# Attention with a low-rank mixer and an MLP on one core: diagonal score blocks first, early key copies, column groups, and transposes of q, k and u by DMA

## Chip, cores, metric

One core of one Trainium2 chip. The metric is the device time of one execution in microseconds (us). Each version was run several times, beside runs of the kernel before on the same chip. A run over 1.5% above the fastest of its kernel counts as slow.

Names: PE is TensorE, the matrix engine; DVE, ACT and POOL are VectorE, ScalarE and GpSimd; SP (SyncE) here only issues DMAs, as POOL does for the loads. SBUF is the on-chip memory for tiles, PSUM the one that PE writes its results to, from where ACT or DVE copy them out.

## The reference, cut to what matters

```python
# q, k, v: (4 batches, 8 heads, 768, 64), float32
scores = q @ k^T / 8 + bias            # keep: key in the first 8, or 0 <= row - column < 96
a      = softmax(scores)               # bias = -slope[head] * distance
x      = (a @ v), heads side by side   # (4, 768, 512)
h      = (x^T @ U @ V)^T               # mixes rows; rank 32
u      = x + h
out    = u + relu(u @ w_ch1) @ w_ch2   # 512 -> 2048 -> 512
```

Because of the band, a query block of 128 rows needs only two key blocks: its own (the "diagonal" block) and the one before, into whose first 32 rows the global keys are copied.

## The kernel before

Heads are worked in pairs: 4 pairs a batch, 16 in all. `kT` and `qT` hold keys and queries transposed, `kP` is the key copy for the previous blocks with the global keys put in, `vp` the same for v. Matrix products take fp16. After pair 3, MLP "units" (four matmuls of 512 columns) of the finished batch are put between the steps of the next pairs: `fill(f)` issues `f` of them, and a pair has eight such slots. What matters below is that DMAs put on one queue are issued in the order of the program: in the timeline after, the transposes of pair 8 come out behind its vp copies (from 84.89 us to 88.96 us).

```python
ORDER = [(1, t) for t in range(1, NSB)] + [(0, t) for t in range(1, NSB)] + [(0, 0)]   # 1: needs kP
CH = [list(range(0, 4)), list(range(4, 8)), list(range(8, 11))]      # three groups of score blocks

def transposes(i, which):               # q or k of pair i: 12 PE transposes of 128 x 64
    ...
        nc.tensor.matmul(tp[64*hi:64*hi+64, sb*P:(sb+1)*P], stg[:, hi, sb], ident16, is_transpose=True, ...)
    ...                                 # qT copied out of PSUM by ACT, kT by DVE

def v_prev(i):                          # vp of pair i, on the SP queue; waits for v
    nc.sync.dma_start(vp[G:P], vh[G:P, :, 0:NPB]); ...   # 3 DMAs

def mix_tmp(i):                         # U-product: accumulates into 32 partitions
    for c in range(NSB):
        nc.tensor.matmul(tmp_ps[0:R], u16[:, c], x16[:, c], start=(c == 0), stop=(c == NSB - 1))
    nc.vector.tensor_copy(tmp16, tmp_ps[0:R])

def mix_t(i):                           # u transposed: 6 PE transposes, copied to uT by DVE
    ...

for i in range(NPAIR, NP):              # pairs 4 to 15
    v_prev(i + 2)
    scores(i + 1, 0)
    fill(f)
    av(i)
    norm(i)
    fill(f)
    scores(i + 1, 1)
    cast_x(i)                           # ACT: x to fp16
    fill(f)
    mask(i + 1, 0)
    transposes(i + 2, 0)
    fill(f)
    mix_tmp(i)
    scores(i + 1, 2)
    fill(f)
    mix_h(i, nc.gpsimd)                 # V-product, u = x + h, cast to fp16
    fill(f)
    transposes(i + 2, 1)
    mask(i + 1, 1)
    k_prev(i + 2, nc.gpsimd)            # kP of pair i + 2
    fill(f)
    if i % 2 == 0 and i + 4 < NP:
        load(i + 4, 2)                  # q, k, v of two pairs, on the POOL queue, cast to fp16
    mix_t(i)
    ...
    fill(f)
```

The softmax here doesn't subtract the row's maximum and nothing guards it: scores larger than these inputs give would overflow.

Of the kernel before, what the change touches and what calls it, by code (L numbers as in the profile page):

```python
# [10 lines left out]
FP16 = mybir.dt.float16  # L11
I32 = mybir.dt.int32
AF = mybir.ActivationFunctionType
ALU = mybir.AluOpType
# [3 lines left out]
def kernel(  # L18
# [13 lines left out]
    nc = tc.nc  # L32
# [14 lines left out]
    TT = 512  # L47
    D1 = D + 1
    KEEP = False
    assert NG <= G and NL <= P - G + 1 and NPAIR == NDC  # L50
    qk_scale = 1.0 / math.sqrt(D)
    BIG = -30000.0
# [1 line left out]

    cst = ctx.enter_context(tc.tile_pool(name="cst", bufs=1))
    big = ctx.enter_context(tc.tile_pool(name="big", bufs=1))
    stp = ctx.enter_context(tc.tile_pool(name="stp", bufs=6))
    qkp = ctx.enter_context(tc.tile_pool(name="qkp", bufs=3))
    epp = ctx.enter_context(tc.tile_pool(name="epp", bufs=2))
    smp = ctx.enter_context(tc.tile_pool(name="smp", bufs=2))  # L60
# [14 lines left out]
    def ps_tp(name, dtype, cols):  # L75
        return psum.tile([P, cols], dtype, name=name, tag="tp", bufs=1)
# [10 lines left out]
    vp16 = big.tile([P, VPR, 2, NPB, D1], FP16, name="vp16")  # L87

    NP = B * NPAIR
    stage = {}  # L90
    xs = {}

# [12 lines left out]
    def load_v(i0, n):  # L105
# [5 lines left out]
            .rearrange("(m p) d -> p m d", p=P),  # L111
        )

    def load(i0, n):
        load_qk(i0, n)
        load_v(i0, n)

    w1v = moe_w_ch1.rearrange("(c p) n -> p c n", p=P)
# [24 lines left out]
    nc.gpsimd.iota(reli, pattern=[[-1, 2 * P]], base=0, channel_multiplier=1)  # L143
    load_v(0, 1)
    load(1, 1)
    load(2, 2)
    u16 = cst.tile([P, NSB, R], FP16, name="u16")
    nc.gpsimd.dma_start(u16, moe_U.rearrange("(c p) r -> p c r", p=P))
    v16w = cst.tile([R, S], FP16, name="v16w")
    nc.gpsimd.dma_start(v16w, moe_V)  # L150
    load_w1()


# [32 lines left out]
    u16s = {}  # L186
    obs = {}
    tmps = {}
    NSTART = NPAIR + 2

    def transposes(i, which):
        if i >= NP:
            return
        stg = stage.pop((i, which))
        if i < NSTART:
            bank = ps_mm("tpb")
            keep_busy(bank, 8 if i == 0 and which == 0 else 1)
            tp = bank.bitcast(FP16)[:, 0:NSB * P]
        else:
            tp = ps_tp("tp", FP16, NSB * P)  # L200
        for sb in range(NSB):
            for hi in range(2):
                nc.tensor.matmul(  # L203
                    tp[64 * hi:64 * hi + 64, sb * P:(sb + 1) * P], stg[:, hi, sb],
                    ident16, is_transpose=True,
                    start=(sb == 0), stop=(sb == NSB - 1),
                )
        tv = tp.rearrange("p (n c) -> p c n", n=NSB)
        if which == 0:
            qT = qkp.tile([P, S], FP16, name="qT", tag="qT")  # L210
            nc.scalar.activation(qT.rearrange("p (c n) -> p c n", n=NSB), tv, AF.Copy)  # L211
            qTs[i] = qT
        else:
            kT = qkp.tile([P, NSB, P], FP16, name="kT", tag="kT")
            nc.vector.tensor_copy(  # L215
                kT.rearrange("p n c -> p (n c)").rearrange("p (c n) -> p c n", n=NSB), tv,
            )
            kTs[i] = kT

    def k_prev(i, eng):  # L220
# [21 lines left out]
                )  # L242


    ORDER = [(1, t) for t in range(1, NSB)] + [(0, t) for t in range(1, NSB)] + [(0, 0)]
    CH = [list(range(0, 4)), list(range(4, 8)), list(range(8, 11))]

    def scores(i, ci):
        if i >= NP:
            return  # L250
        qT, kT, kP = qTs[i], kTs[i], kPs[i]
        if ci == 0:
            probs[i] = epp.tile([P, 2, NBK, P], FP16, name="ep", tag="ep")
        ep = probs[i]
        idx = CH[ci]
        n = len(idx)
        scs = [ps_sc("sc") for _ in range(2)]
        if i < NPAIR:
            keep_busy(scs[0], 1)
        for j, bi in enumerate(idx):  # L260
            prev, t = ORDER[bi]
            for hi in range(2):
                r = slice(64 * hi, 64 * hi + 64)
                lhsT = kP[r, t - 1] if prev else kT[r, t]
                nc.tensor.matmul(  # L265
                    scs[hi][:, j * P:(j + 1) * P], lhsT, qT[r, t * P:(t + 1) * P],
                    start=(j == 0), stop=(j == n - 1),
                )
        for hi in range(2):
            nc.scalar.activation(  # L270
                ep[:, hi, idx[0]:idx[0] + n].rearrange("p n c -> p (n c)"),
                scs[hi][:, 0:n * P], AF.Exp, scale=qk_scale,
            )

    def mask(i, part):
        if i >= NP:
            return
        hp = i % NPAIR
        ep = probs[i]
        eb = expb[:, 2 * hp:2 * hp + 2]  # L280
        j0, m = ((0, 2), (NPB, 1))[part]
        blk = ep[:, :, j0:j0 + NPB]
        nc.vector.tensor_tensor(  # L283
            blk, blk, eb[:, :, m:m + 1].broadcast_to((P, 2, NPB, P)), ALU.mult,
        )
        if part == 1:
            nc.vector.tensor_tensor(
                ep[:, :, NBK - 1], ep[:, :, NBK - 1], eb[:, :, 0], ALU.mult
            )

    def av(i):
        obs[i] = ps_ob("ob")
        ep = probs.pop(i)
        for hi in range(2):
            ob = obs[i][:, 512 * hi:512 * hi + NSB * D1].rearrange("p (n d) -> p n d", n=NSB)
            for t in range(NSB):
                if t == 0:
                    nc.tensor.matmul(
                        ob[:, 0], ep[:, hi, NBK - 1], v16[:, i % VR, hi, 0],
                        start=True, stop=True,  # L300
                    )
                    continue
                nc.tensor.matmul(  # L303
                    ob[:, t], ep[:, hi, t - 1], vp16[:, i % VPR, hi, t - 1],
                    start=True, stop=False,
                )
                nc.tensor.matmul(  # L307
                    ob[:, t], ep[:, hi, NPB + t - 1], v16[:, i % VR, hi, t],
                    start=False, stop=True,
                )  # L310

# [20 lines left out]
    def mix_tmp(i):  # L332
        x16 = x16s.pop(i)
        tmp_ps = ps_tp("tmp_ps", FP32, P)
        for c in range(NSB):
            nc.tensor.matmul(  # L336
                tmp_ps[0:R], u16[:, c], x16[:, c], start=(c == 0), stop=(c == NSB - 1),
            )
        tmp16 = smp.tile([R, P], FP16, name="tmp16", tag="tmp16")
        nc.vector.tensor_copy(tmp16, tmp_ps[0:R])  # L340
        tmps[i] = tmp16

    def mix_h(i, eng):
# [16 lines left out]
    def mix_t(i):  # L360
        b, hp = divmod(i, NPAIR)
        uu = u16s.pop(i)
        tpu = ps_tp("tpu", FP16, S)
        for st in range(NSB):
            nc.tensor.matmul(
                tpu[:, st * P:(st + 1) * P], uu[:, st], ident16, is_transpose=True,
                start=(st == 0), stop=(st == NSB - 1),
            )
        nc.vector.tensor_copy(uT[:, hp, b * S:(b + 1) * S], tpu)
# [66 lines left out]
    for i in range(NPAIR):  # L436
        last = i == NPAIR - 1
        v_prev(i + 2)
        scores(i + 1, 0)
        av(i)  # L440
        norm(i)
        scores(i + 1, 1)
        if i > 0:
            mix_t(i - 1)
        cast_x(i)
        mask(i + 1, 0)
        if not last:
            transposes(i + 2, 0)
            mix_tmp(i)
            scores(i + 1, 2)  # L450
            transposes(i + 2, 1)
            mix_h(i, nc.vector if i == 0 else nc.gpsimd)
            if i + 2 < NPAIR:
                masks_of(i + 2)
            if i == 0:
                v_prev(1)
            mask(i + 1, 1)
            k_prev(i + 2, nc.vector if i == 0 else nc.gpsimd)
        else:
            mix_tmp(i)  # L460
            scores(i + 1, 2)
            mix_h(i, nc.vector)
            transposes(i + 2, 0)
            transposes(i + 2, 1)
            mix_t(i)
            mask(i + 1, 1)
            k_prev(i + 2, nc.gpsimd)
        if i == 0:
            load(4, 2)
        if i == 1:  # L470
            load_w2()
        if i == 2:
            load(6, 2)
# [7 lines left out]

    for i in range(NPAIR, NP):
        if i % NPAIR == 0:
            f = max(1, len(mlp_q) // (8 * NPAIR))
        v_prev(i + 2)
        scores(i + 1, 0)
        fill(f)
        av(i)
        norm(i)
        fill(f)  # L490
        scores(i + 1, 1)
        cast_x(i)
        fill(f)
        mask(i + 1, 0)
        transposes(i + 2, 0)
        fill(f)
        mix_tmp(i)
        scores(i + 1, 2)
        fill(f)
        mix_h(i, nc.gpsimd)  # L500
        fill(f)
        transposes(i + 2, 1)
        mask(i + 1, 1)
        k_prev(i + 2, nc.gpsimd)
        fill(f)
        if i % 2 == 0 and i + 4 < NP:
            load(i + 4, 2)
        mix_t(i)
        if i % NPAIR == NPAIR - 1:
            queue_batch(i // NPAIR)  # L510
        fill(f)
# [37 lines left out]
```

## Time and profile before

| | before |
|---|---|
| median | 291.84 us (3 runs, 290.54 to 291.88) |
| span of the profiled run | 289.3 us |

From the profile page of the kernel before, the busy times and two rows of the span in 40 slices (each digit the busy share of one slice in tenths; PEclk the granted TensorE clock):

```profile
PE 252.7 (87%) x2144; PEld 129.0 (45%) x2144; DVE 149.3 (52%) x239; ACT 104.4 (36%) x185; POOL 61.2 (21%) x80
...
PE   2564585698899999999999999988999999999994
...
PEclk9999999999999999999999999999999999999998
```

PE is the busiest engine, but not evenly. The windows view of the same kernel cuts the span into five stages: the start (pairs 0 to 3 without MLP), pairs 4 to 7, 8 to 11, 12 to 15, and the tail of MLP alone. Columns: window, its length, busy us (and instructions) of PE, PEld (weight loads), DVE, ACT, POOL, then granted clock, DMA share, GB/s.

```profile
0.00:58.70 58.70, 32.76 (x423) 24.23 (x424) 34.43 (x64) 27.12 (x49) 25.02 (x36) 1.00 1.28 165
58.70:111.40 52.70, 49.58 (x482) 24.52 (x481) 31.41 (x48) 23.90 (x43) 14.79 (x18) 1.00 0.59 78
111.40:184.00 72.60, 72.25 (x597) 34.88 (x596) 39.21 (x60) 26.55 (x48) 14.80 (x18) 1.00 0.45 70
184.00:228.50 44.50, 41.37 (x391) 20.57 (x390) 26.99 (x42) 17.23 (x31) 6.64 (x8) 1.00 0.10 33
228.50:289.30 60.80, 56.70 (x257) 24.81 (x255) 17.28 (x25) 9.55 (x16) 0.00 (x0) 0.98 0.11 39
```

In the start PE is busy 32.8 of 58.7 us: it waits. In the three stages of pairs 4 to 15 it is busy 93 to over 99% of the time. Pairs 4 to 7 and 12 to 15 have one unit per slot, pairs 8 to 11 two.

The waits of PE in the start, before (engine, line, who was waited for: us in sum, times, longest):

```profile
PE sc L265 <- POOL kP L226: 8.4, 3, 3.4
PE sc L265 <- DVE kP L226: 6.8, 3, 3.6
```

The first score group needs kP, which is made last. The waits of the SP queue, before: SP stands still for v, at the vp copies, for a quarter of the span.

```profile
SPq L238 <- DMA v_84<-in_v_dram: 69.3, 4, 19.1
```

Last, PE's timeline in one pair of 4 to 7, before (start, duration, line, operation; in brackets the idle time before it and who ended it):

```profile
78.94 0.49 PE L336 MATMUL tmp_ps<-x_1024,u_111 128*32 128x128 f16 x6 [0.69 <-ACT qT L211]
79.37 0.34 PE L265 MATMUL sc<-qT,kT 64*128 64x128 f16 x6
79.64 1.04 PE L381 MATMUL hps<-uT,w_16_81 128*128 128x512 f16 x4
80.61 0.50 PE L348 MATMUL h_ps<-tmp_1061,v16w 32*128 32x128 f16 x6
81.05 1.04 PE L381 MATMUL hps<-uT,w_16_81 128*128 128x512 f16 x4
82.01 0.53 PE L203 MATMUL tp<-ident_93,qkst 128*64 128x128 f16 x12
82.47 1.04 PE L381 MATMUL hps<-uT,w_16_81 128*128 128x512 f16 x4
```

The modelled durations overlap, so the cost of a group is read from start to start: the U-product took 0.43 us (79.37 - 78.94), the V-product 0.44, twelve k transposes 0.46. PE waited 0.69 us ahead of the U-product here.

### The profile page before, as it was taken

The numbers are of one execution on the slowest core, as the hardware profiler recorded it, in microseconds if no ns is written. First come the engines' busy times: TensorE is split into PE (matmuls) and PEld (weight loads), VectorE is DVE, ScalarE is ACT, GpSimd is POOL, SyncE is SP. The second block draws the span as 40 slices with busy tenths as digits, with TensorE's granted clock in tenths as the row PEclk, the third lists the DMA queues.
The fourth block names the chain that finished last, engine by engine and source line by source line (L and its number), as shares of the span: only waits on it lengthen the run. The fifth ranks groups of instructions, "written<-read, shape, count | busy, mean of one in ns | idle before, by whom it ended". The sixth has DMA issues, their size and how long they took to land.

```text
span 289.3 us, 5035 instructions
## 1 busy us (share of the span) xinstructions
PE 252.7 (87%) x2144; PEld 129.0 (45%) x2144; DVE 149.3 (52%) x239; ACT 104.4 (36%) x185; POOL 61.2 (21%) x80
## 2 busy tenths in 40 slices
PE   2564585698899999999999999988999999999994
PEld 1343464454444444444444444544444444444441
DVE  5646736736665665564554635666655432123221
ACT  2753552444644234533146331446431032013100
POOL 8820137102430721060200701120301100000000
PEclk9999999999999999999999999999999999999998
DMA  8999979960971294039120291200011200210021
GB/s 86 176 191 211 175 98 192 191 71 6 125 64 39 30 207 107 2 39 162 73 81 4 21 180 73 69 18 2 0 39 37 75 0 0 75 73 0 0 73 74
DMA packets 47975, 22.68 MB, mean 78 GB/s; under 512 B 31408, under 2 KB 44368, under 8 KB 47952
## 3 DMA queue, kind: packets, MB, share of 16 engines
q0 software_dynamic: 36656, 13.73, 41.1%
q1 hardware_dynamic: 11296, 8.63, 10.2%
q8 instruction: 17, 0.28, 0.4%
q14 instruction: 6, 0.05, 0.1%
HBM read 27.46 MB, written 6.29 MB: 117 GB/s over the span
## 4 chain that ended last, share of the span: by engine, by line
PE 64%; DVE 11%; ACT 10%; POOL 8%; DMA 3%; issue 2%; POOLq 0%; DVEq 0%
PE cps L399 25%; PE hps L381 21%; PE sc L265 6%; ACT ep L270 4%; DVE kT L215 4%; DMA u_111<-in_moe_U_dram 3%; DVE x_sb L353 3%; PE tmp_ps L336 3%; POOL kP L225 3%; PE h_ps L348 2%; PE ob L303 2%; PE ob L307 2%; ACT qT L211 1%; POOL qkst L98 1%; POOL uu L357 1%
## 5 line engine op out<-in xcount | busy, mean ns | idle before, releaser
L381 PE MATMUL hps<-uT,w_16_81 128*128 128x512 f16 x384 | 94.1, 383 | 0.4
L399 PE MATMUL cps<-w_16_82,htr 128*128 128x512 f16 x384 | 90.4, 380 | 0.0
L270 ACT ACTIVATE ep<-sc 128x512 f16<-128x512 f32 (+1 forms) x96 | 48.7, 560 | 90.0 <-PE sc L265 90.0
L381 PEld LDWEIGHTS <-w_16_81 128*128 128x128 f16 x384 | 34.2, 98 | 40.2 <-issue 5.1
L399 PEld LDWEIGHTS <-htr 128*128 128x128 f16 x384 | 34.4, 98 | 38.5
L386 ACT ACTIVATE htr<-hps 128x512 f16<-128x512 f32 x48 | 28.7, 598 | 62.5 <-PE hps L381 61.9
L388 DVE TENSOR_SCALAR htr<-hps 128x512 f16<-128x512 f32 x48 | 33.0, 688 | 34.6 <-PE hps L381 34.6
L357 POOL CAST uu<-x_sb 128x768 f16<-128x768 f32 x14 | 13.1, 935 | 146.9 <-DVE x_sb L353 146.9
L406 DVE TENSOR_TENSOR osb<-cps,x_sb 128x512 f32<-128x512 f32 x24 | 16.6, 690 | 34.0 <-PE cps L399 34.0
L283 DVE TENSOR_TENSOR ep<-ep,expb 128x1280 f16<-128x1280 f16 x32 | 26.2, 818 | 7.4 <-ACT ep L270 7.4
L265 PE MATMUL sc<-qT,kP 64*128 64x128 f16 x160 | 11.6, 249 | 16.2 <-POOL kP L226 8.4
L353 DVE TENSOR_TENSOR x_sb<-x_sb,h_ps 128x768 f32<-128x768 f32 x16 | 15.2, 951 | 16.6 <-PE h_ps L348 16.6
L203 PEld LDWEIGHTS <-qkst 128*64 128x64 f16 x384 | 14.6, 130 | 15.8 <-issue 10.2
L265 PEld LDWEIGHTS <-kP 64*128 64x128 f16 x160 | 5.9, 104 | 27.6 <-POOL kP L226 13.0
L319 DVE RECIPROCAL rcp<-ob 128x12 f32<-128x12 f32 x16 | 3.7, 232 | 25.2 <-PE ob L307 25.2
L225 POOL COPY kP<-kT 128x480 f16<-128x480 f16 x13 | 13.0, 1000 | 15.4 <-DVE kT L215 15.4
L320 DVE TENSOR_TENSOR x_sb<-ob,rcp 128x768 f32<-128x768 f32 x16 | 15.3, 957 | 0.6
L303 PE MATMUL ob<-vp_85,ep 128*128 128x65 f16 x160 | 15.0, 209 | 0.0
L307 PE MATMUL ob<-v_84,ep 128*128 128x65 f16 x160 | 14.9, 209 | 0.0
L203 PE MATMUL tpb<-ident_93,qkst 128*64 128x128 f16 x144 | 10.0, 314 | 5.3 <-DMA qkst<-in_q_dram 4.8
L303 PEld LDWEIGHTS <-ep 128*128 128x128 f16 x160 | 13.1, 108 | 1.6 <-issue 0.3
L307 PEld LDWEIGHTS <-ep 128*128 128x128 f16 x160 | 13.2, 109 | 0.0
(112 smaller groups left out, 204.1 us busy)
## 6 DMA issues: line engine op xcount, KB each, us to landing
out_dram<-osb SPq DMA_DIRECT2D x24, 256.0 KB, 2.0
qkst<-in_q_dram POOLq DMA_DIRECT2D x7, 384.0 KB, 5.6
qkst<-in_k_dram POOLq DMA_DIRECT2D x7, 384.0 KB, 8.3
v_84<-in_v_dram POOLq DMA_DIRECT2D x7, 384.0 KB, 11.3
w_16_81<-in_moe_w_ch_dram POOLq DMA_DIRECT2D x2, 1024.0 KB, 15.8
w_16_82<-in_moe_w_ch_dram POOLq DMA_DIRECT2D x2, 1024.0 KB, 13.4
vp_85<-v_84 SPq DMA_DIRECT2D x14, 121.9 KB, 3.0
vp_85<-v_84 SPq DMA_DIRECT2D x28, 20.3 KB, 2.5
```

What stands on the lines that cost most here:

```text
L203: nc.tensor.matmul(tp[64 * hi:64 * hi + 64, sb * P:(sb + 1) * P], stg[:, hi, sb], ident16, is_transpose=True, start=(sb == 0), stop=(sb == ...
L225: eng.tensor_copy(kP[:, :, G:P], kT[:, 0:NPB, G:P])
L265: nc.tensor.matmul(scs[hi][:, j * P:(j + 1) * P], lhsT, qT[r, t * P:(t + 1) * P], start=(j == 0), stop=(j == n - 1),)
L270: nc.scalar.activation(ep[:, hi, idx[0]:idx[0] + n].rearrange("p n c -> p (n c)"), scs[hi][:, 0:n * P], AF.Exp, scale=qk_scale,)
L283: nc.vector.tensor_tensor(blk, blk, eb[:, :, m:m + 1].broadcast_to((P, 2, NPB, P)), ALU.mult,)
L303: nc.tensor.matmul(ob[:, t], ep[:, hi, t - 1], vp16[:, i % VPR, hi, t - 1], start=True, stop=False,)
L307: nc.tensor.matmul(ob[:, t], ep[:, hi, NPB + t - 1], v16[:, i % VR, hi, t], start=False, stop=True,)
L353: nc.vector.tensor_tensor(xp, xp, hps[:, 0:S].rearrange("p (n c) -> p n c", n=NSB), ALU.add)
L381: nc.tensor.matmul(hh, w1_16[:, dc, jt * P:(jt + 1) * P], uT[:, dc, t0:t0 + TT], start=(dc == 0), stop=(dc == NDC - 1),)
L386: nc.scalar.activation(htr[:, jt], hh, AF.Relu)
L388: nc.vector.tensor_scalar_max(htr[:, jt], hh, 0.0)
L399: nc.tensor.matmul(cps, htr[:, jc, tt * P:(tt + 1) * P], w2_16[:, jc], start=(jc == 0), stop=(jc == NJC - 1),)
```

## The change

The intent: take work off PE, which bounds pairs 4 to 15, and shorten the chain that bounds the start. Diagonal blocks need only kT, so they go first and kP may come later. kT is copied by ACT. The U-product goes to four column groups of the array, and the V-product then sums over 128 instead of 32 partitions. q and k from pair 6 on, and u from batch 1 on, are transposed by DMA from one SBUF tile to another; for that q and k are loaded row by row, into four buffers.

```diff
+    NSTART = NPAIR + 2
+    def load_qk_natural(i):
+        for which, src in enumerate((q, k)):
+            stg = stp.tile([P, NSB, 2, D], FP16, name="qkn", tag="qkn", bufs=4)
+            for hi in range(2):
+                nc.gpsimd.dma_start(stg[:, :, hi], src[b, 2*hp + hi].rearrange("(n p) d -> p n d", p=P))
...
     def transposes(i, which):
+        if DT and i >= NSTART:
+            dst = qkp.tile([P, NSB, P], FP16, name="qkT", tag="qT" if which == 0 else "kT")
+            nc.sync.dma_start_transpose(dst, stg.rearrange("p n h d -> p (n h d)"))
+            ...
+            return
...
-            nc.vector.tensor_copy(kT..., tv)
+            nc.scalar.activation(ko, tv, AF.Copy)        # but pair 0
...
-    ORDER = [(1, t) for t in range(1, NSB)] + [(0, t) for t in range(1, NSB)] + [(0, 0)]
+    ORDER = [(0, t) for t in range(1, NSB)] + [(0, 0)] + [(1, t) for t in range(1, NSB)]
...
-                tmp_ps[0:R], u16[:, c], x16[:, c], start=(c == 0), stop=(c == NSB - 1),
+                tmp_ps[g*R:(g+1)*R], u16[:, c], x16[:, c], start=(c < NGR), stop=(c + NGR >= NSB),
+                tile_position=(0, g*R),                  # g = c % 4; V is copied to all four groups
...
     def mix_t(i):
+        if DT and i >= NPAIR:
+            nc.sync.dma_start_transpose(uT[:, hp, b*S:(b+1)*S]..., uu...)
+            return
...
     for i in range(NPAIR, NP):
         v_prev(i + 2)
         scores(i + 1, 0); fill(f); av(i); norm(i)
+        transposes(i + 2, 0)
         fill(f)
         scores(i + 1, 1); cast_x(i); fill(f); mask(i + 1, 0)
-        transposes(i + 2, 0)
-        fill(f)
         mix_tmp(i)
+        fill(f)
         scores(i + 1, 2); fill(f)
-        mix_h(i, nc.gpsimd)
-        fill(f)
-        transposes(i + 2, 1)
-        mask(i + 1, 1)
+        mix_h(i, nc.vector if DT else nc.gpsimd)
+        mask(i + 1, 1)
+        transposes(i + 2, 1)
         k_prev(i + 2, nc.gpsimd); fill(f); load(...)
+        fill(f)
         mix_t(i)
```

In the start, the same order of scores is used, masks come before the work on u, and U and V are loaded before pairs 2 and 3.

More of the change, by code (lines that the diff above doesn't have):

```diff
@@ L49 @@
     KEEP = False
+    DT = True
     assert NG <= G and NL <= P - G + 1 and NPAIR == NDC
@@ L56 @@
     big = ctx.enter_context(tc.tile_pool(name="big", bufs=1))
-    stp = ctx.enter_context(tc.tile_pool(name="stp", bufs=6))
+    stp = ctx.enter_context(tc.tile_pool(name="stp", bufs=4))
     qkp = ctx.enter_context(tc.tile_pool(name="qkp", bufs=3))
@@ L112, in load_v @@
         )
-    def load(i0, n):
-        load_qk(i0, n)
+    def load_qk_natural(i):
+        b, hp = divmod(i, NPAIR)
+        for which, src in enumerate((q, k)):
+            stg = stp.tile([P, NSB, 2, D], FP16, name="qkn", tag="qkn", bufs=4)
+            for hi in range(2):
+                nc.gpsimd.dma_start(
+                    stg[:, :, hi],
+                    src[b, 2 * hp + hi].rearrange("(n p) d -> p n d", p=P),
+                )
+            stage[i, which] = stg
+    def load(i0, n):
+        if DT and i0 >= NSTART:
+            for j in range(n):
+                load_qk_natural(i0 + j)
+        else:
+            load_qk(i0, n)
         load_v(i0, n)
@@ L145 @@
     load(1, 1)
-    load(2, 2)
     u16 = cst.tile([P, NSB, R], FP16, name="u16")
     nc.gpsimd.dma_start(u16, moe_U.rearrange("(c p) r -> p c r", p=P))
-    v16w = cst.tile([R, S], FP16, name="v16w")
-    nc.gpsimd.dma_start(v16w, moe_V)
+    NGR = P // R
+    v16w = cst.tile([P, S], FP16, name="v16w")
+    nc.gpsimd.dma_start(v16w[0:R], moe_V)
+    for g in range(1, NGR):
+        nc.sync.dma_start(v16w[g * R:(g + 1) * R], v16w[0:R])
+    load(2, 2)
     load_w1()
@@ L188 @@
     tmps = {}
-    NSTART = NPAIR + 2
     def transposes(i, which):
@@ L194, in transposes @@
         stg = stage.pop((i, which))
+        if DT and i >= NSTART:
+            dst = qkp.tile([P, NSB, P], FP16, name="qkT", tag="qT" if which == 0 else "kT")
+            nc.sync.dma_start_transpose(dst, stg.rearrange("p n h d -> p (n h d)"))
+            if which == 0:
+                qTs[i] = dst.rearrange("p n c -> p (n c)")
+            else:
+                kTs[i] = dst
+            return
         if i < NSTART:
@@ L214, in transposes @@
             kT = qkp.tile([P, NSB, P], FP16, name="kT", tag="kT")
-            nc.vector.tensor_copy(
-                kT.rearrange("p n c -> p (n c)").rearrange("p (c n) -> p c n", n=NSB), tv,
-            )
+            ko = kT.rearrange("p n c -> p (n c)").rearrange("p (c n) -> p c n", n=NSB)
+            if i == 0:
+                nc.vector.tensor_copy(ko, tv)
+            else:
+                nc.scalar.activation(ko, tv, AF.Copy)
             kTs[i] = kT
@@ L250, in scores @@
             return
-        qT, kT, kP = qTs[i], kTs[i], kPs[i]
+        qT, kT, kP = qTs[i], kTs[i], kPs.get(i)
         if ci == 0:
@@ L280, in mask @@
         eb = expb[:, 2 * hp:2 * hp + 2]
-        j0, m = ((0, 2), (NPB, 1))[part]
+        j0, m = ((0, 1), (NSB, 2))[part]
         blk = ep[:, :, j0:j0 + NPB]
@@ L285, in mask @@
         )
-        if part == 1:
+        if part == 0:
             nc.vector.tensor_tensor(
-                ep[:, :, NBK - 1], ep[:, :, NBK - 1], eb[:, :, 0], ALU.mult
+                ep[:, :, NPB], ep[:, :, NPB], eb[:, :, 0], ALU.mult
             )
@@ L298, in av @@
                     nc.tensor.matmul(
-                        ob[:, 0], ep[:, hi, NBK - 1], v16[:, i % VR, hi, 0],
+                        ob[:, 0], ep[:, hi, NPB], v16[:, i % VR, hi, 0],
                         start=True, stop=True,
@@ L303, in av @@
                 nc.tensor.matmul(
-                    ob[:, t], ep[:, hi, t - 1], vp16[:, i % VPR, hi, t - 1],
+                    ob[:, t], ep[:, hi, NSB + t - 1], vp16[:, i % VPR, hi, t - 1],
                     start=True, stop=False,
@@ L307, in av @@
                 nc.tensor.matmul(
-                    ob[:, t], ep[:, hi, NPB + t - 1], v16[:, i % VR, hi, t],
+                    ob[:, t], ep[:, hi, t - 1], v16[:, i % VR, hi, t],
                     start=False, stop=True,
@@ L335, in mix_tmp @@
         for c in range(NSB):
+            g = c % NGR
             nc.tensor.matmul(
-                tmp_ps[0:R], u16[:, c], x16[:, c], start=(c == 0), stop=(c == NSB - 1),
-            )
-        tmp16 = smp.tile([R, P], FP16, name="tmp16", tag="tmp16")
-        nc.vector.tensor_copy(tmp16, tmp_ps[0:R])
+                tmp_ps[g * R:(g + 1) * R], u16[:, c], x16[:, c],
+                start=(c < NGR), stop=(c + NGR >= NSB),
+                tile_position=(0, g * R),
+            )
+        tmp16 = smp.tile([P, P], FP16, name="tmp16", tag="tmp16")
+        nc.vector.tensor_copy(tmp16, tmp_ps)
         tmps[i] = tmp16
@@ L362, in mix_t @@
         uu = u16s.pop(i)
+        if DT and i >= NPAIR:
+            nc.sync.dma_start_transpose(
+                uT[:, hp, b * S:(b + 1) * S].rearrange("p (n c) -> p n c", n=NSB),
+                uu.rearrange("p n c -> p (n c)"),
+            )
+            return
         tpu = ps_tp("tpu", FP16, S)
@@ L442 @@
         scores(i + 1, 1)
+        cast_x(i)
+        mask(i + 1, 0)
+        if i == 0:
+            v_prev(1)
+        transposes(i + 2, 0)
         if i > 0:
             mix_t(i - 1)
-        cast_x(i)
-        mask(i + 1, 0)
-        if not last:
-            transposes(i + 2, 0)
-            mix_tmp(i)
-            scores(i + 1, 2)
-            transposes(i + 2, 1)
-            mix_h(i, nc.vector if i == 0 else nc.gpsimd)
+        mix_tmp(i)
+        scores(i + 1, 2)
+        if last:
+            mix_h(i, nc.vector)
+            mask(i + 1, 1)
+            transposes(i + 2, 1)
+            k_prev(i + 2, nc.gpsimd)
+            mix_t(i)
+        else:
+            transposes(i + 2, 1)
+            k_prev(i + 2, nc.vector if i == 0 else nc.gpsimd)
+            mask(i + 1, 1)
+            mix_h(i, nc.vector)
             if i + 2 < NPAIR:
                 masks_of(i + 2)
-            if i == 0:
-                v_prev(1)
-            mask(i + 1, 1)
-            k_prev(i + 2, nc.vector if i == 0 else nc.gpsimd)
-        else:
-            mix_tmp(i)
-            scores(i + 1, 2)
-            mix_h(i, nc.vector)
-            transposes(i + 2, 0)
-            transposes(i + 2, 1)
-            mix_t(i)
-            mask(i + 1, 1)
-            k_prev(i + 2, nc.gpsimd)
         if i == 0:
@@ L489 @@
         norm(i)
+        transposes(i + 2, 0)
         fill(f)
@@ L494 @@
         mask(i + 1, 0)
-        transposes(i + 2, 0)
+        mix_tmp(i)
         fill(f)
-        mix_tmp(i)
         scores(i + 1, 2)
         fill(f)
-        mix_h(i, nc.gpsimd)
-        fill(f)
+        mix_h(i, nc.vector if DT else nc.gpsimd)
+        mask(i + 1, 1)
         transposes(i + 2, 1)
-        mask(i + 1, 1)
         k_prev(i + 2, nc.gpsimd)
```

## The prediction

> **What bounds the kernel now.** Three stretches (busy time by windows, and the timeline). (a) 0 to 58 us: pairs 0 to 3, no MLP. PE is busy 8.4, 12.5 and 13.1 us of each 20; a pair takes about 10.6 us. A latency chain: in PE's waits, the scores wait 13.7 us for kP (five times), the key copy that DVE and POOL make last. (b) 58 to 228 us: pairs 4 to 15 with MLP units between. PE is busy 19 to 20 of 20 us: PE bound. A pair takes 12.4 us at one unit per slot (pairs 4-7, 12-15), 18.4 us at two. (c) 228 to 289 us: MLP alone, PE bound, untouched by the change.
>
> **What the change removes.** Per pair in (b), by start-to-start times in the timeline: two groups of 12 q/k transposes, 0.46 us each; 6 u-transposes, about 0.4 us with the waits around them; the U and V products (about 0.4 us each with switches of array shape) lose perhaps 0.3 us together; the small waits for qT, kT and kP (4.1 us over pairs 4-7). Estimate: 2.2 us a pair at one unit, 1.8 at two: 8 x 2.2 + 4 x 1.8 = 25 us.
> In (a) scores start from kT, kT is copied on ACT, the mask comes before the u work, and U arrives earlier (now 3% of the chain). The remaining chain adds up to about 8 us a pair: about 10 us less.
>
> **What it adds.** (1) q/k of pair 6 on are loaded row by row: 6144 packets for two pairs instead of 1024. A 256-byte-source packet takes 32 ns here, a 1536-byte-source one 79 ns; v's 3072 packets land about 3.4 us after k's. So a two-pair load grows from about 9 to about 14 us (estimate). (2) 32 DMA transposes on the SP queue, in order with the vp copies, whose issue costs 0.62 us each, and the outputs. The trace has no such transpose; the Trainium skill ("VectorE: DVE Perf Modes", The three transpose paths) gives 1309 ns for 128x128; I guess 3 to 5 us to landing for 128x768.
>
> **What is given back.** On SP the transposes of pair i+2 stand behind vp(i+2), which waits for v; v is now issued after the row-by-row loads, and half of these wait for buffers freed by earlier transposes. SP already waited 69.3 us for v, in four waits. In (a) the DMA engines are 90% busy, so v of pairs 6/7 will land near 62 us, as before, while PE would be ready for pair 6's scores near 59: a stall of 5 to 10 us around pair 5. Another 3 to 5 us with the next load, and 2 to 3 us at the last u-transposes before the tail, where u's DMA latency is exposed. Sum: -35 + 15 = -20, less some doubt about DMA latency.
>
> **Predicted: 274 us, range 262 to 289.** Faster by over 2%: 0.81; within 2%: 0.08; slower: 0.11.
>
> **What would show it.** Pair time in (a) about 8 us and no kP wait; first MLP unit near 49 us; pairs 8-11 about 16.6 us, 12-15 about 10.3 us; tail still about 60.6 us; new PE waits, "sc" on DMA qT/kT, around pairs 5 and 7; less DVE and ACT busy time.
>
> **What would make it wrong.** DMA transposes that occupy SP or the DMA engines for 8 us or more each: three a pair would then set the pair time, and the kernel would be far slower. Or no stalls: then about 264 us.

## More of the kernel before

One reading of PEclk needs care. The first four hidden-layer matmuls of the kernel before took 1.89 us:

```profile
58.68 1.89 PE L381 MATMUL hps<-uT,w_16_81 128*128 128x512 f16 x4
```

Four of the same took 1.04 us later (79.64 us above), yet PEclk reads 1.00 at both times. The first clock record of this trace is at 62.2 us, so the view's 1.00 before that time is no measurement.

## The result and the profile after

| | median | runs | ratio to before |
|---|---|---|---|
| before | 291.75 us | 4, 290.54 to 291.88 | |
| changed | 282.04 us | 4, 281.28 to 282.55 | 0.9674 (95%: 0.9639 to 0.9708) |

A ratio is the mean time of one kernel's fast runs over that of the other's of the same rounds, so it is not quite the ratio of the medians quoted. The result is correct, and 3.3% faster.

The same lines of the page, after:

```profile
PE 234.0 (84%) x1832; PEld 116.4 (42%) x1832; DVE 134.0 (48%) x226; ACT 100.6 (36%) x180; POOL 68.9 (25%) x96
...
PE   2567786976785898999999999678989899999994
...
PEclk9999998699999799999999999999999999999999
```

PE lost 18.7 us of busy time (252.7 to 234.0), but the span only 9.3. Its share fell: new holes stand in slices 8 to 15 (counted from 0) and again in 25 and 26, and PEclk drops in slices 6, 7 and 13. The drop in slices 6 and 7 is not new: the kernel before had slow matmuls at the same point of its work, the first MLP units, without a clock record. The one in slice 13 is new. The windows by stage, after, with the same columns:

```profile
0.00:49.30 49.30, 30.79 (x422) 22.24 (x422) 29.62 (x61) 30.56 (x54) 24.43 (x36) 0.98 1.33 177
49.30:107.30 58.00, 44.70 (x364) 21.02 (x363) 27.53 (x45) 21.23 (x39) 21.49 (x28) 0.93 1.21 123
107.30:176.50 69.20, 65.68 (x477) 30.73 (x476) 35.06 (x56) 23.73 (x43) 21.32 (x29) 1.00 0.95 108
176.50:218.20 41.70, 36.12 (x320) 17.61 (x319) 24.51 (x40) 15.53 (x28) 1.70 (x4) 1.00 0.44 76
218.20:280.05 61.85, 56.75 (x257) 24.81 (x255) 17.29 (x25) 9.55 (x16) 0.00 (x0) 0.99 0.12 42
```

| stage | before | after | difference |
|---|---|---|---|
| start | 58.7 | 49.3 | -9.4 |
| pairs 4 to 7 | 52.7 | 58.0 | +5.3 |
| pairs 8 to 11 | 72.6 | 69.2 | -3.4 |
| pairs 12 to 15 | 44.5 | 41.7 | -2.8 |
| tail | 60.8 | 61.85 | +1.0 |

The whole gain is the start. From pair 4 on, where the DMA transposes act, gains and losses cancel. The waits of PE from 49 to 228 us, after, show three kinds that the kernel before does not have from pair 4 on: for DMA transposes, for ACT and DVE to empty the PSUM of the hidden layer ("htr", 4.8 us in two lines), and for the cast of x. (The last line stands for eight of its kind, one a pair, 6.8 us in sum.)

```profile
PE sc L295 <- DMA qkT<-qkn: 7.6, 4, 3.6
PE hps L420 <- DMA uT<-uu: 3.4, 3, 1.2
PE hps L420 <- ACT htr L425: 3.1, 6, 0.7
PE hps L420 <- DVE htr L427: 1.7, 2, 1.0
PE tmp_ps L367 <- ACT x_855 L359: 0.9, 1, 0.9
```

The SP queue's waits, after: still 64.1 us for v, and new ones at the uT transposes. (The engine named for those is the one that came last by the trace; what the DMA needs is the cast u.)

```profile
SPq L268 <- DMA v_84<-in_v_dram: 64.1, 7, 15.4
SPq L397 <- DVE ep L313: 18.8, 6, 5.4
```

The largest hole is seen in the timeline of all engines, after, between 77 and 92 us:

```profile
77.69 1.45 POOL L110 DMA_DIRECT2D v_84<-in_v_dram  x1
...
82.52 0.29 PE L367 MATMUL tmp_ps<-x_1153,u_106 128*32 128x128 f16 x6 [0.93 <-ACT x_1153 L359]
82.74 1.04 PE L438 MATMUL cps<-w_16_82,htr 128*128 128x512 f16 x4
...
84.89 0.62 SPq L268 DMA_DIRECT2D vp_85<-v_84  x1
...
85.19 2.75 PE L438 MATMUL cps<-w_16_82,htr 128*128 128x512 f16 x12
...
86.92 1.23 SPq L217 DMA_TRANSPOSE qkT<-qkn  x1
...
88.96 1.26 SPq L217 DMA_TRANSPOSE qkT<-qkn  x1
...
91.50 0.52 PE L295 MATMUL sc<-qkT 64*128 64x128 f16 x8 [3.55 <-DMA qkT<-qkn]
...
91.95 1.89 PE L438 MATMUL cps<-w_16_82,htr 128*128 128x512 f16 x4
```

Read it backwards. PE stood 3.55 us for the transposed k of pair 8. SP issued the transposes of q and k at 86.92 and 88.96, each 1.2 us long, behind the vp copies of pair 8 (an output stands between the two), which had stood in SP's order since v was late: v was issued only at 77.69. In the last line four matmuls take 1.89 us where four such took 1.04 at 82.74 us: after the idle stretch the clock was down (0.52 from 91.5 to 95 us). The Trainium skill ("TensorE: Matmul & The Clock Gate", What's actually happening) has the array throttled after an idle window of about 3.4 us; this gap of 3.55 us agrees, but shorter gaps throttled it too in other runs (see the end). At 82.52 stands a second new wait, 0.93 us for the cast of x.

The DMA transposes themselves are quick in this kernel. From the list of DMA issues, after (count, median us from issue to landing):

```profile
qkT<-qkn SPq DMA_TRANSPOSE x20, 3.2
uT<-uu SPq DMA_TRANSPOSE x12, 2.8
```

### The profile page after: what moved, and what is told of

It reads as the page before. It is cut to its first block, busy times and chain, and to the rows that moved or that the text cites. A ratio compares the mean times of both kernels' runs of the same rounds, so it can differ in the third digit from the quotient of the medians.

```text
span 280.0 us, 4506 instructions
## 1 busy us (share of the span) xinstructions
PE 234.0 (84%) x1832; PEld 116.4 (42%) x1832; DVE 134.0 (48%) x226; ACT 100.6 (36%) x180; POOL 68.9 (25%) x96
## 4 chain that ended last, share of the span: by engine, by line
PE 59%; DMA 15%; ACT 11%; DVE 7%; POOL 3%; issue 2%; SPq 2%; DVEq 0%; ACTq 0%; POOLq 0%
PE cps L438 24%; PE hps L420 24%; DMA w_16_82<-in_moe_w_ch_dram 6%; ACT ep L300 6%; PE sc L295 4%; DMA uT<-uu 3%; DMA qkT<-qkn 3%; DVE x_sb L386 2%; DMA qkst<-in_q_dram 2%; DVE ep L313 2%; PE ob L333 2%; PE ob L337 2%; PE tmp_ps L367 1%; PE h_ps L381 1%; ACT htr L425 1%
## 5 line engine op out<-in xcount | busy, mean ns | idle before, releaser
L420 PEld LDWEIGHTS <-w_16_81 128*128 128x128 f16 x384 | 35.2, 98 | 49.8 <-issue 13.9
L438 PEld LDWEIGHTS <-htr 128*128 128x128 f16 x384 | 35.3, 98 | 40.2 <-issue 0.9
L121 POOL DMA_DIRECT2D qkn<-in_k_dram x20 | 16.6, 842 | 23.0 <-DMA qkT<-qkn 17.7
L255 POOL COPY kP<-qkT 128x480 f16<-128x480 f16 x10 | 6.3, 634 | 64.4 <-DMA qkT<-qkn 58.6
L121 POOL DMA_DIRECT2D qkn<-in_q_dram x20 | 17.0, 860 | 17.0 <-DMA qkT<-qkn 17.0
L386 DVE TENSOR_TENSOR x_sb<-x_sb,h_ps 128x768 f32<-128x768 f32 x16 | 15.2, 952 | 11.6 <-PE h_ps L381 11.6
L333 PE MATMUL ob<-vp_85,ep 128*128 128x65 f16 x160 | 15.5, 212 | 1.1 <-DVE ep L313 1.1
L337 PE MATMUL ob<-v_84,ep 128*128 128x65 f16 x160 | 15.5, 212 | 0.0
L333 PEld LDWEIGHTS <-ep 128*128 128x128 f16 x160 | 13.5, 110 | 4.4 <-issue 1.6
L337 PEld LDWEIGHTS <-ep 128*128 128x128 f16 x160 | 13.6, 111 | 0.0
L295 PE MATMUL sc<-qkT 64*128 64x128 f16 x120 | 7.0, 223 | 7.6 <-DMA qkT<-qkn 7.6
L110 POOL DMA_DIRECT2D v_84<-in_v_dram x9 | 12.3, 1370 | 0.0
## 6 DMA issues: line engine op xcount, KB each, us to landing
w_16_82<-in_moe_w_ch_dram POOLq DMA_DIRECT2D x2, 1024.0 KB, 15.2
```

The source lines that it names most:

```text
L121: nc.gpsimd.dma_start(stg[:, :, hi], src[b, 2 * hp + hi].rearrange("(n p) d -> p n d", p=P),)
L295: nc.tensor.matmul(scs[hi][:, j * P:(j + 1) * P], lhsT, qT[r, t * P:(t + 1) * P], start=(j == 0), stop=(j == n - 1),)
L333: nc.tensor.matmul(ob[:, t], ep[:, hi, NSB + t - 1], vp16[:, i % VPR, hi, t - 1], start=True, stop=False,)
L337: nc.tensor.matmul(ob[:, t], ep[:, hi, t - 1], v16[:, i % VR, hi, t], start=False, stop=True,)
L386: nc.vector.tensor_tensor(xp, xp, hps[:, 0:S].rearrange("p (n c) -> p n c", n=NSB), ALU.add)
L420: nc.tensor.matmul(hh, w1_16[:, dc, jt * P:(jt + 1) * P], uT[:, dc, t0:t0 + TT], start=(dc == 0), stop=(dc == NDC - 1),)
```

## The experiments

Ratios are to the kernel before: its medians were 290.37 us (e1 to e4), 291.17 (e5 to e8), 290.35 (e9 to e12). All results were correct. The diffs are shortened: the runs used flags in place of `False`. The table gives the mean of each kernel's fast runs, and differences between two kernels below are taken from it; the text of each run gives the median of all its runs. The stages come from one profile each; e4 and e7 are left out because their profiled runs were slow (one and one run; e6 had one slow run, e10 three); their fast means are 281.5 and 276.6 us. The kernel before had fast means of 291.5, 290.2, 290.7 and 290.6 us in the four calls, so a difference between kernels of different calls is uncertain by about 1 us; by the ratios the changed kernel is 4.2 us behind e3, where the means say 5.2.

| | fast mean | ratio | start | pairs 4-7 | 8-11 | 12-15 | tail |
|---|---|---|---|---|---|---|---|
| changed | 281.98 | 0.9674 | 49.3 | 58.0 | 69.2 | 41.7 | 61.8 |
| e1 no DMA transpose | 281.38 | 0.9689 | 49.5 | 52.6 | 72.8 | 44.0 | 60.5 |
| e2 only u by DMA | 282.06 | 0.9709 | 50.0 | 53.9 | 71.7 | 43.0 | 62.1 |
| e3 only q, k by DMA | 276.79 | 0.9531 | 48.7 | 53.1 | 69.2 | 42.1 | 60.8 |
| e5 = e3 + slot moved | 272.65 | 0.9371 | 50.0 | 51.2 | 68.7 | 39.7 | 60.8 |
| e6 changed, vp behind transposes | 275.66 | 0.9478 | 48.7 | 52.4 | 70.0 | 40.7 | 61.8 |
| e8 = e1 + row loads | 280.72 | 0.9648 | 48.7 | 52.1 | 72.9 | 43.9 | 60.5 |
| e9 = e5 + vp behind | 264.74 | 0.9104 | 49.8 | 45.7 | 68.7 | 38.1 | 60.8 |
| e10 = e9 + u by DMA | 270.02 | 0.9285 | 49.9 | 48.7 | 70.9 | 38.5 | 61.9 |
| e11 = e10, last pair's u on PE | 265.67 | 0.9138 | 49.8 | 47.0 | 68.1 | 37.7 | 60.7 |
| e12 = e1 + slot moved | 274.42 | 0.9437 | 49.0 | 49.5 | 72.8 | 40.4 | 60.6 |

### First call: undo parts

**e1_no_dma_transpose.** Everything but the DMA transposes.

```diff
-        if DT and i0 >= NSTART:        # loads
+        if False and i0 >= NSTART:
-        if DT and i >= NSTART:         # q, k
+        if False and i >= NSTART:
-        if DT and i >= NPAIR:          # u
+        if False and i >= NPAIR:
-    stp ... bufs=4
+    stp ... bufs=6
```

> All of the change except the DMA transposes: q, k and u are transposed on PE throughout, q and k are loaded as before, 6 staging buffers as before; the u cast stays on DVE. Theory A (the prediction: the DMA transposes are worth some 10 us net after their stalls): about 290 us, that is 8 us or more slower than the changed kernel's 282. Theory B (the DMA transposes gain nothing, because the stalls of pairs 4 to 7 eat what PE saves; the gain is the start's): 279 to 283 us, start up to the first MLP unit about 49 us, pairs 4 to 7 about 49 us instead of 56.5, pairs 8 to 11 about 72 us, pairs 12 to 15 about 46 us.

281.26 us (281.15 to 281.86), ratio 0.9689 (0.9669 to 0.9709), the same as the changed kernel's 0.9674. Theory B holds for the total (its figure for pairs 4 to 7, 49 us, was missed): in this order of steps all DMA transposes together are worth nothing. They take pairs 4 to 7 from 52.6 to 58.0 us and give 3.6 and 2.3 us back in the later pairs. Moreover e1 gains nothing over the kernel before from pair 4 on, although its U-product is cheaper. Its PE waits from 48 us on name the reason:

```profile
PE tmp_ps L369 <- ACT x L361: 7.0, 8, 0.9
```

**e2_only_u_by_dma.** As e1, but u of pairs 4 to 15 by DMA.

> The changed kernel with only u transposed by DMA; q and k on PE from rows loaded as before. Theory B, with the harm in the q/k part (row-by-row loads, buffers, order on SP): faster than the changed kernel by 2 to 6 us, about 277 us: no PE wait for qkT, pairs 4 to 7 about 48 us; the wait for uT at the batch ends (3.4 us in the changed kernel) stays. Theory A: slower than the changed kernel by some 5 us, since the q/k transposes are 11 us of PE.

282.41 us, ratio 0.9709 (0.9674 to 0.9745). Both theories missed: u by DMA alone has no q/k stall, and yet gains nothing on e1. Its trace has 7.0 us of waits for the cast, as e1, and 2.7 us for uT.

**e3_only_qk_by_dma.** The changed kernel with u of all pairs on PE.

```diff
-        if DT and i >= NPAIR:          # u
+        if False and i >= NPAIR:
```

> The changed kernel with only q and k transposed by DMA, u on PE. Theory B: the stall of pairs 4 to 7 stays (56 us for these pairs), PE takes back 12 x 0.4 us: 284 to 287 us. Rival for the stall: it is the uT DMA ahead in the SP queue, which waits for the u cast, that delays the q/k transposes; then this kernel loses that wait and pairs 4 to 7 take about 50 us, total about 278 us.

277.02 us (275.69 to 277.43), ratio 0.9531 (0.9502 to 0.9560): 4 to 5 us faster than the changed kernel. The rival was right in the total, though pairs 4 to 7 took 53.1 us, not 50. The traces show the path: in the changed kernel the first uT transpose stands in SP between the transposes of pair 6 and the vp copies of pair 7. Without it the transposes of pair 7 are issued at 65.8 instead of 68.2 us, their buffers come free, v of pairs 8 and 9 is issued at 74.4 instead of 77.7, and the vp copies of pair 8 start at 80.8 instead of 84.9. (1.1 us of this lead is there before the first uT transpose.) The stall at pair 8 is gone; that at pair 6 (2.9 us) stays.

**e4_fill_before_uprod.** The changed kernel with one slot moved.

```diff
         mask(i + 1, 0)
+        fill(f)
         mix_tmp(i)
-        fill(f)
         scores(i + 1, 2)
```

> The changed kernel with one MLP slot moved back ahead of the U-product, where it stood before the change. In the changed kernel PE waits 0.9 us for the cast of x in most pairs with one unit per slot (0.9 us seven times from pair 4 on), a wait that the removed q transposes used to cover. If those waits are on the chain: 4 to 6 us faster, about 277 us. If the pair's time is set elsewhere (the q/k transposes, the SP queue) then within 1.5 us of the changed kernel.

282.79 us, ratio 0.9694 (0.9623 to 0.9765), runs from 278.98 to 284.01. No gain that these runs resolve. That fits the second reading, that SP sets the time; a trace of a fast run that would show it is lacking.

### Second call: order on SP, slot, first pair, loads

**e5_qk_by_dma_fill_moved.** e3 with the slot moved as in e4.

> The kernel with only q and k by DMA (277.0 us) plus the MLP slot moved back ahead of the U-product. There PE still waits 4.7 us from pair 4 on for the cast of x before the U-product. If this wait is on the chain now that the u DMA is gone: 3 to 5 us faster, 272 to 274 us, with no wait of the U-product for the cast from pair 4 on. If moving the slot only shifts the wait to the scores or the hidden layer, as it did in the changed kernel: 276 to 278 us.

272.32 us, ratio 0.9371 (0.9323 to 0.9418): 4 to 5 us faster than e3. With u off SP, the cast wait is on the chain, and moving the slot takes it away: from pair 4 on the trace of e3 has 7.0 us of it, that of e5 none.

**e6_vp_behind_transposes.** The changed kernel with another order on SP.

```diff
     for i in range(NPAIR, NP):
-        v_prev(i + 2)
         scores(i + 1, 0)
...
         transposes(i + 2, 1)
+        v_prev(i + 2)
         k_prev(i + 2, nc.gpsimd)
```

> The changed kernel with the copies of v's rows (vp of pair i+2) put behind the two q/k transposes of pair i+2 on the SP queue, from pair 4 on; all data and loads the same. Theory (head-of-line blocking: the transposes wait behind vp, which waits for v, which is loaded last): SP no longer holds the transposes of pairs 6 and 8 until v has landed, the pair times of 16.2 and 15.0 us fall towards 12, PE waits less than 2 us for qkT instead of 7.6: 275 to 278 us. Rival (the q/k rows themselves or the DMA engines are late, so that the order on SP does not matter): within 1.5 us of the changed kernel, 281 to 283 us.

275.77 us, ratio 0.9478 (0.9425 to 0.9531); one of the four runs was slow, 281.54. Same loads, same DMA work, other order: 6 us faster. The PE waits of e6 after 48 us show the stall for q and k gone and the one for uT grown:

```profile
PE hps L420 <- DMA uT<-uu: 6.2, 3, 2.9
...
PE sc L295 <- DMA qkT<-qkn: 0.6, 1, 0.6
```

**e7_dma_from_pair_8.** The changed kernel, but q and k of pairs 6 and 7 are loaded and transposed as before.

> The changed kernel with DMA transposes of q and k from pair 8 on instead of pair 6; pairs 6 and 7 loaded and transposed on PE as before. If the first stall (pair 4 to 5, 16.2 us) comes from loading pair 6 and 7 row by row behind the second weights: this interval falls to about 13.5 us while PE takes back 4 x 0.46 us; about 280 us, and the granted clock no longer drops. If the stall only moves to pair 8: about 282 us or more.

277.19 us (275.41 to 279.55), ratio 0.9506 (0.9434 to 0.9579). Faster than expected, but with a wide spread. The profile fell on a slow run, so how much of it is the first stall is left open; e6 reaches a like time without putting the work of these two pairs back on PE.

**e8_row_loads_pe_transposes.** e1 with the row-by-row loads and buffers of the changed kernel, transposed on PE (the copies out of PSUM are then plain).

> The kernel without DMA transposes (281.3 us), but with q and k of pair 6 on loaded row by row, in the same tiles and buffers as in the changed kernel, and transposed on PE. It measures the row-by-row loads by themselves. If the extra packets or their issue on POOL harm: pairs 4 to 7 take 53 us or more instead of 51, total 284 us or more. If the loads are harmless without the SP queue's waits: 280 to 282 us.

280.83 us, ratio 0.9648 (0.9607 to 0.9689). The loads by themselves cost nothing that shows. What harm they do in the changed kernel needs something that waits behind them.

### Third call: all mended, and what is left

**e9_qk_dma_fill_vp.** The edits of e3, e4 and e6 together.

> Only q and k by DMA, the MLP slot back ahead of the U-product, and vp behind the transposes on SP. The three losses that the earlier runs named are then all out. If they add up: 277.0 - 4.7 (slot) - 4 (stall of pair 6's scores) = 268 to 270 us, pairs 4 to 7 about 46 us in sum with no wait for qkT over 1 us. If the stall is partly hidden elsewhere: 271 to 273 us.

264.74 us (263.84 to 265.76, 6 runs), ratio 0.9104 (0.9076 to 0.9133). Better than expected: 9% faster than before, and 17 us faster than the changed kernel. Windows of the stages from pair 4 to the tail, e9:

```profile
49.80:95.50 45.70, 43.65 (x387) 21.47 (x386) 28.25 (x49) 21.12 (x39) 21.11 (x28) 0.97 1.46 132
95.50:164.20 68.70, 66.29 (x503) 31.96 (x502) 36.65 (x60) 23.39 (x43) 22.06 (x29) 1.00 0.95 102
164.20:202.30 38.10, 37.52 (x343) 18.81 (x342) 25.81 (x44) 15.76 (x29) 1.70 (x4) 1.00 0.39 67
```

Its PE waits from 49 to 228 us, and SP's wait for v:

```profile
PE hps L422 <- ACT htr L427: 1.9, 6, 0.6
PE sc L297 <- POOL kP L258: 1.3, 2, 1.1
PE hps L422 <- DVE htr L429: 1.3, 2, 0.6
```

```profile
SPq L270 <- DMA v<-in_v_dram: 35.8, 6, 14.3
```

SP still waits for v, but nothing that PE needs soon stands behind it. What is left are waits for the hidden layer's PSUM to be emptied (lines "hps", 3.2 us) and for kP.

**e10_u_dma_mended.** e9 with u by DMA as in the changed kernel.

> The same with u by DMA as well, as in the changed kernel. Two things can make u by DMA a loss: its place in the SP queue, where it waits for the u cast with the next pair's vp and transposes behind it, and its landing time at the end of a batch, where the hidden layer waits for it. With vp moved the first should be small; PE waits 5 to 7 us for uT at the batch ends, against 12 x 0.4 = 5 us of PE saved: 269 to 273 us, no better than with u on PE.

273.41 us (267.78 to 275.71), but three of its six runs were slow; the fast ones give the ratio 0.9285 (0.9230 to 0.9341) and are 5.3 us slower than e9. Its profiled run, a fast one of 269.9 us span, has these PE waits from 48 us on (the longest two lines). The expectation, no better than with u on PE, is met.

```profile
PE hps L422 <- DMA uT<-uu: 4.6, 3, 2.1
PE hps L422 <- ACT htr L427: 3.9, 6, 0.7
```

**e11_u_dma_but_last.** e10, but u of the last pair of each batch on PE.

```diff
-        if DT and i >= NPAIR:
+        if DT and i >= NPAIR and hp != NPAIR - 1:
```

> The same, but u of the last pair of each batch stays on PE. If the loss of u by DMA is the exposed landing at the batch ends, this kernel has no PE wait for uT and is the fastest: 2 to 4 us faster than with all of u by DMA and 1 to 3 us faster than with none, 266 to 269 us. If the loss is the SP queue, it equals the kernel with all of u by DMA or is slower than the one with none.

265.53 us (264.83 to 266.83), ratio 0.9138 (0.9107 to 0.9169). The loss of e10 is gone, and so are the waits for uT: it was u of the last pair, whose landing is exposed at the batch ends, where the hidden layer of the next batch needs u at once. The expectation's other half missed: u by DMA elsewhere does not beat e9. Against e9, pairs 8 to 11 gain 0.6 us and pairs 4 to 7 lose 1.3 (the scores wait 2.9 us for kP, in e9 1.3).

**e12_no_dma_transpose_fill.** e1 with the slot moved.

> The kernel without any DMA transpose (281.3 us) with the MLP slot back ahead of the U-product. It says what the U-product in column groups is worth when PE does not wait for the cast (7 to 8 us of such waits in 281.3), and what q/k by DMA are worth in the mended order. If the wait is on the chain: 275 to 278 us, and then q/k by DMA are worth about 7 us. If another wait takes its place: 280 to 281 us.

274.23 us, ratio 0.9437 (0.9408 to 0.9466): 7 us faster than e1, and faster than the change as made. e9 against e12 (264.7 and 274.4) says that DMA transposes of q and k are worth 9.7 us once the order is right. The PE time of these transposes, ten pairs at 1.0 us, is about as much. (e9 also has vp behind the transposes; without DMA transposes that was not tried.)

## Why the prediction was right or wrong

The measured 282.0 us lies in the range of 262 to 289, and "faster by over 2%" came true. The stated 274 was 8 us too low: of a forecast gain of 17.8 us 9.7 came, and a range 27 us wide took that in. The start, and not the balance of the pairs, is what carried it: from pair 4 to the end the forecast was 10 us less and the profiles show none.

- **The start: right.** "About 10 us less" was 9.4. The first MLP unit came at 49.3 us (predicted near 49), the second and third pair took 8.1 to 8.2 us (the first 9.7), and the waits for kP in the start are down from 15.2 us to none. Which of the start's edits brought it, no run separates; all runs keep them, and take 48.7 to 50.0 us.
- **Where the stalls are, and why: right.** The prediction put the transposes of pair i+2 behind vp and v on SP, with stalls around pair 5 and with the next load. The A·V of pair 5 started 16.2 us after that of pair 4, and that of pair 7 15.0 us after pair 6; in e9 these steps are 12.3 and 10.4: 3.9 and 4.6 us, where 5 to 10 and 3 to 5 were predicted. e6 shows the cause by moving only vp.
- **The DMA transposes: right, in part by what stood before them.** 3.2 and 2.8 us to landing (guessed 3 to 5) in the changed kernel, where they stand behind the vp copies, and so behind v. With the vp copies moved behind them some start while the load is still under way (e9 issued one at 53.3 us; it landed at 60.7, v at 62.2), and those of q and k take 6.0 us in e6, 4.5 in e9 and 5.9 in e10 (medians; 8.8 at most). The Trainium skill ("VectorE: DVE Perf Modes", The three transpose paths) has 1309 ns for one 128x128 block; no run measures one block, but six blocks in one DMA take 3.2 us here, and not six times that.
- **The gain per pair: mis-sized.** "2.2 us a pair at one unit, 1.8 at two: 25 us". With the losses mended (e9) the three stages with pairs 4 to 15 shrink from 169.8 to 152.5 us, so 17.3 us. Most of the missing 7.7 us are two terms. u: e9 leaves it on PE, and 12 x 0.4 us of the 25 are u's; e11, with nine of its twelve by DMA, gains 17.0 us, no more. And q/k were counted in twelve pairs, but the trace of the kernel before has them in ten (240 transposes from pair 4 on, 48 of them in pairs 12 to 15), 1.8 us too much. Without these two the estimate is 18.4 us. The prediction for two units per slot has a further error, which the other pairs make up in part. For pairs 8 to 11 the start-to-start times of PE's groups, summed from the trace, tell which term was off:

| pairs 8 to 11, us | before | after | e9 |
|---|---|---|---|
| q/k transposes | 4.00 | 0 | 0 |
| u transposes | 1.34 | 0 | 1.34 |
| U-product | 1.76 | 1.42 | 0.89 |
| V-product | 1.75 | 1.34 | 1.34 |
| hidden-layer units | 28.26 | 31.13 | 30.23 |

  The PE work came off as costed: 1.0 us for q and k, 0.33 for u, 0.2 and 0.1 for the U- and V-products. (The 1.42 us after hold about 0.5 us of waits of the group that follows.) The halved U-product fits the Trainium skill ("TensorEngine Tiling (Array Packing)", When to Use Tiling): a stationary operand of 32 columns, as U's is, allows four column tiles. But the hidden-layer units grew by 2 to 3 us. That is what the waits view shows over this stage: 2.4 us in e9 and 2.1 us after for ACT and DVE, which empty the PSUM of these units, and after another 1.2 us for uT; before, PE waits for nothing here. e12 has 2.0 us of these waits without any DMA transpose, so they come from other parts of the change (the order of steps, the cast of u on DVE); no run says from which. "PE bound" was taken to mean that every us off PE is a us off the time.
- **What is given back: one part missed, one too small.** The prediction counted SP's stalls and 2 to 3 us of u's latency at the tail. It did not see that the removed q transposes, and the slot that stood behind them, had covered the cast of x: 0.9 us a pair at one unit, worth 4 to 5 us (e3 to e5) or 7 us (e1 to e12). And u by DMA costs, at the batch ends and by its place on SP, about 5 us in sum (4.2 to 5.2 from the changed kernel to e3, 5.3 from e9 to e10). These overlap; in sum the changed kernel is 17.2 us behind e9, against 15 predicted.

So the term that failed most is the 25 us: gains of 17 and losses of 17 leave nothing from pair 4 on, and the measured gain is the start's.

Left open: why half of e10's runs were slow, how much of e7's gain is the first stall, which of the start's edits brought its gain, and what makes the hidden layer wait for its PSUM.

## What to carry to other kernels

When work leaves a full engine, ask what it was hiding: a wait that the removed work covered comes out in its place unless other work is moved there. A transfer put on an in-order queue inherits every wait ahead of it, so put what is needed soonest first and let copies that may be late stand last. Before moving work to DMA, look where its latency ends: in the middle of a batch it changed little here (e11, 0.9 us behind e9), at the batch's end it cost more than it saved.

## What the Trainium skill lacked or had wrong

- "VectorE: DVE Perf Modes" gives the time of a DMA transpose for 128x128 only, and no page has it from issue to landing for a larger one, or beside other loads. A 128x768 fp16 transpose from SBUF to SBUF took 1.2 us on the SP queue and landed after 2.8 to 3.2 us in the changed kernel (medians; 2.5 to 6.2 over all), and 4.5 to 6.0 us for q and k in the kernels that issue it ahead of vp (e6, e9, e10).
- The same page's rule for 128x128 prefers TensorE where PSUM will do as a destination. Here DMA was better for q and k where PE was the bound, by 9.7 us in all (e9 against e12), and not for u (e10, 5.3 us slower than e9). The page lacks the question which engine is the bound and what waits at the end.
- "DMA: Bandwidth & Descriptors" warns of transfers below 512 bytes. Here a 256-byte source row took 32 ns a packet and a 1536-byte one 79 ns (the trace's packet records, kernel before), so a byte cost 2.4 times as much, yet loading q and k row by row did not change the time (e8, 280.7 against 281.4 us).
- "TensorE: Matmul & The Clock Gate" has the array throttled after an idle window of about 3.4 us. Here gaps of PE of 2.13 us (e10, at 167 us), 2.87 us (e6, at 96 us) and 2.94 us (e3, at 62 us) were followed by 3.4 us at a granted 0.5, while one of 2.79 us (after, at 63 us) was not.
- The same page describes the throttled default state. The granted clock in the profile need not show it at the start: in the kernel before it reads 1.00 there, for want of a record until 62.2 us, while the twelve transposes of a group span 0.85 us and later 0.53, and four hidden-layer matmuls 1.89 us and later 1.04. The page has a caveat on such clock events, which does not name this case.
